# C of the first two token pairs: loaded in rows of 512 bytes and turned by VectorE, in a Mamba-2 scan with a feed-forward block

## The chip, the cores and the metric

The kernel runs on one core of a Trainium2 chip. The metric is the device time of one execution in microseconds, here the median of several runs. The core has five engines with a queue of instructions each: TensorE (PE in the profile; PEld is its weight load), VectorE (DVE), ScalarE (ACT), GpSimd (POOL) and SyncE (SP), which here only issues DMAs. SPq and ACTq are the queues of SyncE and ScalarE when they issue a DMA.

## What is computed

A selective state-space scan (Mamba-2) feeds a block of two matrix products with a leaky activation. Cut to what matters:

```python
# x (4, 8, 768, 32); a (4, 8, 768); B, C (4, 8, 768, 16): batch, heads, tokens, width
log_a = np.log(np.clip(a, 1e-06, 1.0))
for c in range(nc):                       # chunks of 32 tokens
    cum = np.cumsum(la, axis=-1)
    L = np.exp(cum[..., :, None] - cum[..., None, :]) * causal
    y_intra = einsum('bhij,bhjd->bhid', einsum('bhin,bhjn->bhij', Cc, Bc) * L, xc)
    y_inter = einsum('bhin,bhnd->bhid', Cc, state) * np.exp(cum)[..., None]
    y[:, :, sl] = y_intra + y_inter
    state = exp(sum la) * state + sum_j exp(cum[-1:] - cum)_j * B_j (x) x_j
h = y_as_(3072, 256) @ w_in               # (256, 2048)
g = np.maximum(h, 0.0) + alpha * np.minimum(h, 0.0)
out = g @ w_out                           # (2048, 256)
```

w_in and w_out arrive as 64-bit floats, which the kernel converts itself.

## The kernel before, in words

The 3072 tokens of all batches are cut into 24 chunks of 128, which are handled in twelve pairs; a group is four chunks, 512 tokens. For each pair the kernel loads B, C and x, forms the decays with scans on VectorE, the products of B and C ("gram") on TensorE, multiplies both, and adds up y from them and from the carried state. The feed-forward block goes over groups. All engines' orders are written out by hand: the order in which the Python code calls operations is the order in each engine's queue, and an engine whose next instruction has to wait holds everything behind it.

The start, up to some 27 us of the profile, is the function `first_two` (L821). It handles pairs 0 and 1 in chunks of 64 tokens, with the first weights' conversion and the first hidden products between them. In the order of the code:

- `load_pair(0)` (L235) issues the first loads. On SyncE: a for the pair (`ap`), B for the pair's two chunks (L192), x for both (L197), a of pair 1. On ScalarE's queue: the rows of a (L184), C for both chunks (L192), alpha. A load of B or C for one chunk takes 128 tokens into 128 partitions and, for each token, eight rows of 16 floats, one for each head: 1024 rows of 64 bytes, 64 KB.
- Two pieces of raw weights (`load_next`, L1435, issued by L257), 512 KB each, follow on SyncE.
- `rows_short` and `rows_out` send small products to DRAM, then `load_pair(1)` (L982) issues B, C, B, C (L192) and x, x (L197), and `load_second` (L983, issued by L231) reads back the products (`ap`).
- VectorE clamps a (L437), scans the rows (L493, L497), and scans the decays of pair 0 out of PSUM (L871, four scans), which TensorE has spread (L865).
- `turned` (L837) turns B and C of pair 0: four transposes on TensorE (L843), with tokens in the partitions before and head and state width after, into two banks, and two copies by ScalarE (L847), C first. `spread_c` (L851, L854) then makes `cz`, C masked by the head's parity, on ScalarE.
- alpha is turned and copied (L992, L994); GpSimd multiplies B by the decays (`bn`, L533).
- gram of pair 0 (L881) needs B's copy and `cz`; VectorE multiplies it into the decays (L887); TensorE adds up y (L929), the states (L895, L910, masked by GpSimd in L916) and their part of y (L941). `cd` (L961) is C times the decays, on GpSimd.
- VectorE and ScalarE convert the first raw piece of w_in (L296, L278, L308; L273, L283), GpSimd adds the halves (L330), and the first hidden products run (L1110).
- Pair 1 goes the same way, with the conversion of further pieces between its steps; its `turned` is at L1040 and its scans at L1029 to L1035, and its gram and y come between the matrix products of the second pair of hidden blocks (`among`, L1062).

Some short matrix products of constants (`keep_warm`, L335) fill TensorE's pauses at the start. Pairs 2 to 4 turn B and C on TensorE (L669). From pair 5 on (`turned` in `load_pair`, which is true from there), B and C are also loaded as blocks of 512 contiguous bytes, 8 tokens of one head to a partition (L210 to L217), and turned by VectorE in blocks of 32 by 32 (`turn_bc`, L571, L574).

The lines around the change in `first_two` are these:

```python
        rows_turn("short", prq)
        tp, hp = spare(), spare()
        bc0 = turned(nat0, (tp, hp), True)
        cz0 = spread_c(bc0)
```

Of the kernel before, what the change touches and what calls it, by code (L numbers as in the profile page):

```python
# [22 lines left out]
def kernel(  # L23
# [25 lines left out]
    nc = tc.nc  # L49
# [4 lines left out]
    batch, H, S, D = x.shape  # L54
    N = B.shape[-1]
    P = 128
    Q = 128
# [18 lines left out]
    NB = 2  # L76
# [20 lines left out]
    gp = ctx.enter_context(tc.tile_pool(name="gp", bufs=16))  # L97
# [6 lines left out]
    def bank(i):  # L104


        return ps_q.tile([P, 512], F32, name="bank", tag=f"q{i}")
# [15 lines left out]
    def load_rows(i, eng=nc.sync):  # L123

        rows = ld.tile([RW, Q], F32, name="rows")
        eng.dma_start(out=rows, in_=a.rearrange("b h (c t) -> (b h c) t", t=Q)[i * RW : (i + 1) * RW])
        loads["r", i] = rows
# [3 lines left out]
    def load_a(t, b, c, eng=nc.sync):  # L131
        first = a[b, 0:1, c * Q : (c + 2) * Q]
        eng.dma_start(out=t, in_=bass.AP(tensor=first.tensor, offset=first.offset,
                                             ap=[[S, H], [0, N], [1, 2 * Q]]))
# [4 lines left out]
    def load_tokens(dst, src, t0):  # L139


        d = dst.rearrange("p j (h w) -> p j h w", h=H)
        for k in range(2):
            for j in range(2):
                t = t0 + k * Q + j * HQ
                nc.sync.dma_start(out=d[HQ * k : HQ * (k + 1), j],
                                  in_=src[:, t : t + HQ, :].rearrange("h p w -> p h w"))

    def load_spread(gp, b, c):

        for w, t in enumerate(loads["p", gp][1] if gp >= HALF else ()):
            rows = scratch["z", b // 2].rearrange("(b h c) t -> b c h t", b=2, h=H)
            for k in range(2):
                nc.sync.dma_start(
                    out=t[HQ * k : HQ * (k + 1), : 4 * SQ].rearrange("p (h t) -> p h t", h=4),
                    in_=rows[b % 2, c + k, 4 * w : 4 * w + 4].unsqueeze(0)
                    .to_broadcast([HQ, 4, SQ]))
        for k, t in enumerate(loads["p", gp][1] if gp < HALF else ()):
            rows = scratch["z", b // 2].rearrange("(b h c) t -> b c h t", b=2, h=H)[b % 2, c + k]
            nc.sync.dma_start(out=t.rearrange("p (h t) -> p h t", h=H),  # L160
                              in_=rows.unsqueeze(0).to_broadcast([P, H, Q]))
            yield

    def load_products(gp, ap):
        b, c = divmod(2 * gp, CPB)
        rows = scratch["pf", b // 2].rearrange("(b h c) t -> b h (c t)", b=2, h=H)
        rows = rows[b % 2, :, c * Q : (c + 2) * Q]
        nc.sync.dma_start(out=ap, in_=rows.unsqueeze(1).to_broadcast([H, N, 2 * Q]))

    def load_pair(gp, decays=True, parted=False):  # L170


        b, c = divmod(2 * gp, CPB)
        turned = gp > GC
        nat = ldx.tile([P, 3, 2, H * N], F32, name="nat")
        xt = ldx.tile([P, 2, HD], F32, name="xt")

        ap = ldx.tile([P, 2 * Q], F32, name="ap")
        if gp == 0:
            load_a(ap, b, c)  # L180
        elif gp > NB:
            load_products(gp, ap)
        if gp == 0:
            load_rows(0, nc.scalar)  # L184
        abc = []
        if gp >= HALF:
            load_tokens(nat[:, 0], B[b], c * Q)
        def load_bc(k):
            ts = slice((c + k) * Q, (c + k + 1) * Q)
            for i, src in enumerate((B,) if turned else (B, C)):  # L190
                eng = nc.scalar if gp == 0 and i else nc.sync
                eng.dma_start(out=nat[:, i, k].rearrange("p (h n) -> p h n", h=H),  # L192
                              in_=src[b, :, ts, :].rearrange("h p n -> p h n"))

        def load_x(k):
            ts = slice((c + k) * Q, (c + k + 1) * Q)
            nc.sync.dma_start(out=xt[:, k].rearrange("p (h d) -> p h d", h=H),  # L197
                              in_=x[b, :, ts, :].rearrange("h p d -> p h d"))

        for k in range((1 if parted else 2) if gp < HALF else 0):  # L200
            load_bc(k)
            if gp >= NB:
                load_x(k)
        for k in range(2 if gp < NB else 0):
            load_x(k)
        if gp == 0:
            nc.scalar.dma_start(out=al_n, in_=moe_alpha.rearrange("(k p) -> k p", p=P))
            loads["a", 1] = prep.tile([P, 2 * Q], F32, name="a1")
            load_a(loads["a", 1], b, c + 2)
        for i, src in enumerate((B, C) if turned else ()):  # L210


            for e in range(2):
                first = src[b, e : e + 1, c * Q : (c + 2) * Q, :]
                nc.sync.dma_start(out=nat[:, 1 + e, i],
                                  in_=bass.AP(tensor=first.tensor, offset=first.offset,
                                              ap=[[2 * S * N, P // 32], [8 * N, 32], [1, 8 * N]]))  # L217
        for k in range(2 if gp >= NB else 0):
            abc.append(lda.tile([P, H * Q], F32, name="abc"))
        loads["p", gp] = nat, abc, xt, ap  # L220
        if gp >= HALF:
            load_tokens(xt, x[b], c * Q)
        if decays:
            for part in load_spread(gp, b, c):
                pass
        return lambda: load_bc(1), lambda: load_x(1)

    def load_second():

        rows = scratch["short", 0].rearrange("(b h c) t -> b h (c t)", b=2, h=H)  # L230
        nc.sync.dma_start(out=loads["p", 1][3], in_=rows[0, :, 2 * Q : 4 * Q].unsqueeze(1)  # L231
                          .to_broadcast([H, N, 2 * Q]))
# [102 lines left out]
    def keep_warm(to, n, cols=2 * Q):  # L335

        for i in range(n):
            nc.tensor.matmul(to[:, :cols], warm.to_broadcast([P, P]), warm.to_broadcast([P, cols]),
                             start=True, stop=True, skip_group_check=True)

    keep_warm(ps_h.tile([P, GT], F32, name="hp"), WARM, GT)
    ident = const.tile([P, P], F32, name="ident")
# [3 lines left out]
    for v in range(2):  # L346
        vs = slice(HQ * v, HQ * (v + 1))
        nc.vector.tensor_copy(out=ident_q[vs].rearrange("p (c t) -> p c t", c=4),
                              in_=ident[vs, vs].unsqueeze(1).to_broadcast([HQ, 4, HQ]))
# [196 lines left out]
    def spare():  # L546

        return ps_h.tile([P, GT], F32, name="hp", tag="hp")
# [272 lines left out]
    def first_two():  # L821
# [4 lines left out]
        nat0, _, xt0, ap0 = loads["p", 0]  # L826
# [7 lines left out]
              for i in range(2)]  # L834
        halves = [slice(HQ * j, HQ * (j + 1)) for j in range(2)]

        def turned(nat, banks, warmed=False):  # L837


            bc = work.tile([P, 4, Q], F32, name="bc")  # L840
            for k in range(2):
                for i, tp in enumerate(banks):
                    nc.tensor.transpose(tp[:, k * P : (k + 1) * P], nat[:, i, k], ident)  # L843
                if warmed and k == 0:
                    keep_warm(banks[0][:, 2 * Q :], 1)
            for i in (1, 0):
                nc.scalar.copy(out=bc[:, 2 * i : 2 * i + 2].rearrange("p k t -> p (k t)"),  # L847
                               in_=banks[i][:, : 2 * Q])
            return bc

        def spread_c(bc):  # L851
            cz = czp.tile([P, 2, 2, Q], F32, name="cz")
            for e in range(2):
                nc.scalar.mul(cz[:, e].rearrange("p k t -> p (k t)"),  # L854
                              bc[:, 2:].rearrange("p k t -> p (k t)"), par[:, e : e + 1])
            return cz
# [13 lines left out]
        def scan(i, r, t):  # L870
            nc.vector.tensor_tensor_scan(out=dec[i][:, r], data0=t[:, : 2 * Q], data1=ident_q,  # L871
                                         initial=0.0, op0=ALU.mult, op1=ALU.add)
# [27 lines left out]
        def dps_in(banks):  # L900
            return [t[:, 2 * Q : 2 * Q + 4 * D].rearrange("p (k m) -> p k m", k=2) for t in banks]
# [54 lines left out]
        def ss():  # L956
            return ps_s.tile([P, 512], F32, name="ss")
# [20 lines left out]
        sp = [bank(r) for r in range(4)]  # L978
# [3 lines left out]
        load_pair(1)  # L982
        load_second()  # L983
        nat1, _, xt1, pf1 = loads["p", 1]
        for r in range(4):
            scan(0, r, sp[r])
        rows_turn("short", prq)
        tp, hp = spare(), spare()
        bc0 = turned(nat0, (tp, hp), True)
        cz0 = spread_c(bc0)  # L990
        al_p = ss()
        nc.tensor.transpose(al_p[:, :NF], al_n, ident[:NF, :NF])  # L992
        keep_warm(al_p[:, Q:], 1, 3 * Q)
# [23 lines left out]
        sp = [bank(r) for r in range(4)]  # L1017
# [19 lines left out]
        convert_next(first=False)  # L1037
        own = [ss(), ss()]
        second = spare()
        bc1 = turned(nat1, (sp[0], second))  # L1040
        cz1 = spread_c(bc1)
        dps = dps_in(own)
        mask(0, slice(3, 4))
        slope_signs()
# [535 lines left out]
```

## Time and profile before

| What | Value |
|---|---|
| runs | 355.82, 355.99, 357.87 us; median 355.99 |
| the profiled execution: its span, first instruction to last | 355.9 us |
| busy: PE, DVE, ACT, POOL | 349.3, 235.8, 171.8, 204.4 us |
| DMA queue of SyncE (q1) | 103048 packets, 29.43 MB |
| DMA queue of ScalarE (q10) | 2496 packets, 0.32 MB |
| load of B or C, 64-byte rows, to issue (L192) | median 526 (B) and 592 ns (C) on SyncE, longest 3521 and 3890 |
| load of B or C, 512-byte rows, to issue (L215) | median 568 and 536 ns |
| VectorE's transpose of 128x512 (L574) | 1112 ns, median of 7 |
| ScalarE's copy of 128x256 out of PSUM (L847) | 373 ns |
| share of the chain that ended last: PE, SPq, DMA, DVE | 89, 4, 3, 2% |

A row of a timeline gives the start and duration in us, the engine, the line of the kernel, the operation, the tile written and the one read, its shape, how many instructions are merged into the row, and in brackets how long the engine was idle before it and what ended that. In a table by stage each engine's busy time in the stretch is followed by the number of its instructions; the last three columns are TensorE's granted clock (1.00 is full), the DMA engines' mean busy share and the GB/s moved. In a list of waits: who waited for whom, us in total, times, the longest.

### The profile page before, as it was taken

The numbers are of one execution on the slowest core, as the hardware profiler recorded it, in microseconds if no ns is written. First come the engines' busy times: TensorE is split into PE (matmuls) and PEld (weight loads), VectorE is DVE, ScalarE is ACT, GpSimd is POOL, SyncE is SP. The second block draws the span as 40 slices with busy tenths as digits, with TensorE's granted clock in tenths as the row PEclk, the third lists the DMA queues.
The fourth block names the chain that finished last, engine by engine and source line by source line (L and its number), as shares of the span: only waits on it lengthen the run. The fifth ranks groups of instructions, "written<-read, shape, count | busy, mean of one in ns | idle before, by whom it ended". The sixth has DMA issues, their size and how long they took to land.

```text
span 355.9 us, 7778 instructions
## 1 busy us (share of the span) xinstructions
PE 349.3 (98%) x2985; PEld 284.4 (80%) x2985; DVE 235.8 (66%) x482; ACT 171.8 (48%) x391; POOL 204.4 (57%) x228
## 2 busy tenths in 40 slices
PE   8899999999999999999999999999999999999996
PEld 4576665578788888888888888888888888888885
DVE  6876986998748756847747856757856633643363
ACT  3477576535355346345345445345445344443431
POOL 6776568589939855725646626637526535434520
PEclk9999999999999999999999999999999999999999
DMA  7899989607345403503423423422001001001102
GB/s 138 182 202 270 329 174 279 148 17 159 106 83 128 102 3 75 104 2 77 78 57 74 86 51 71 85 55 65 11 2 31 0 2 29 2 1 31 31 0 59
DMA packets 105581, 30.24 MB, mean 85 GB/s; under 512 B 79896, under 2 KB 101448, under 8 KB 105544
## 3 DMA queue, kind: packets, MB, share of 16 engines
q1 hardware_dynamic: 103048, 29.43, 36.3%
q10 hardware_dynamic: 2496, 0.32, 0.6%
q8 instruction: 23, 0.38, 0.5%
q14 instruction: 14, 0.11, 0.1%
HBM read 26.32 MB, written 3.42 MB: 84 GB/s over the span
## 4 chain that ended last, share of the span: by engine, by line
PE 89%; SPq 4%; DMA 3%; DVE 2%; ACT 1%; POOL 1%; issue 0%; DVEq 0%; ACTq 0%
PE bank L1216 33%; PE hp L1241 29%; PE bank L1142 6%; PE ss L1241 6%; PE hp L1095 3%; DMA raw<-in_moe_w_in_dram 2%; SPq L192 2%; PE ss L787 1%; PE ss L731 1%; PE hp L1110 1%; PE bank L1209 1%; PE ss L805 1%; PE ss L779 1%; DMA xt<-in_x_dram 1%; SPq L197 1%; PE ss L742 1%
## 5 line engine op out<-in xcount | busy, mean ns | idle before, releaser
L1298 POOL TENSOR_TENSOR gt<-gt 128x512 f32<-128x512 f32 x58 | 74.2, 1279 | 21.1 <-DVE gt L1226 16.3
L1216 PE MATMUL bank<-gt,w_out 128*128 128x256 f32 x320 | 83.5, 381 | 0.0
L1216 PEld LDWEIGHTS bank<-gt,w_out 128*128 128x128 f32 x320 | 60.1, 190 | 9.2 <-issue 1.0
L1288 POOL TENSOR_TENSOR gt<-gt 128x512 f32<-128x512 f32 x20 | 25.4, 1269 | 62.5 <-DVE gt L1226 49.7
L1226 DVE SCALAR_TENSOR_TENSOR gt<-hp,s_mul,gt 128x256 f32<-128x256 f32 x96 | 42.0, 479 | 29.1 <-ACT gt L1224 26.8
L1224 ACT ACTIVATE gt<-hp,s_alpha 128x256 f32<-128x256 f32 x96 | 40.3, 471 | 34.5 <-PE hp L1241 31.4
L1216 PE MATMUL bank<-gt,ws 128*128 128x256 f32 x224 | 55.9, 379 | 0.0
L1216 PEld LDWEIGHTS bank<-gt,ws 128*128 128x128 f32 x224 | 42.3, 190 | 5.6
L1241 PE MATMUL hp<-xs,w_in 128*128 128x256 f32 x160 | 41.9, 384 | 0.0
L1241 PE MATMUL hp<-xs,ws 128*128 128x256 f32 x160 | 41.1, 380 | 0.0
L1267 DVE TENSOR_TENSOR hp<-hp,u 128x512 f32<-128x512 f32 x20 | 14.0, 700 | 35.2 <-ACT u L1265 35.2
L1241 PEld LDWEIGHTS hp<-xs,ws 128*128 128x128 f32 x160 | 30.3, 190 | 4.3 <-POOL xs L1183 0.2
L1241 PEld LDWEIGHTS hp<-xs,w_in 128*128 128x128 f32 x160 | 29.7, 190 | 4.5
L1142 PE MATMUL bank<-w_out,gt 128*128 128x256 f32 x128 | 31.1, 385 | 0.4 <-POOL w_out L330 0.4
L1142 PEld LDWEIGHTS bank<-w_out,gt 128*128 128x128 f32 x128 | 23.6, 190 | 7.2 <-issue 2.9
L1241 PE MATMUL ss<-xT,w_in 128*128 128x256 f32 x96 | 24.6, 379 | 0.0
L645 POOL TENSOR_TENSOR sm<-state,bmask 128x256 f32<-128x256 f32 (+1 forms) x10 | 6.2, 620 | 29.0 <-DVE state L642 29.0
L1095 PE MATMUL hp<-xT,w_in 128*128 128x512 f32 x48 | 22.8, 596 | 0.0
L561 DVE TENSOR_TENSOR_SCAN dec<-abc,bank 128x192 f32<-128x192 f32 x48 | 22.7, 522 | 0.0
L1256 ACT COPY m<-hp 128x512 f32<-128x512 f32 x8 | 4.7, 586 | 35.7 <-PE hp L1241 35.7
L1265 ACT COPY u<-hp 128x512 f32<-128x512 f32 x20 | 11.7, 585 | 19.4 <-PE hp L1241 19.4
L1226 DVE SCALAR_TENSOR_TENSOR gt<-c,s_mul,gt 128x256 f32<-128x256 f32 x40 | 20.6, 555 | 0.0
(232 smaller groups left out, 608.2 us busy)
## 6 DMA issues: line engine op xcount, KB each, us to landing
abc<-z SPq DMA_DIRECT2D x24, 192.0 KB
raw<-in_moe_w_in_dram SPq DMA_DIRECT2D x8, 512.0 KB
raw<-in_moe_w_out_dram SPq DMA_DIRECT2D x8, 512.0 KB
abc<-z SPq DMA_DIRECT2D x8, 512.0 KB
out_dram<-o_sb SPq DMA_DIRECT2D x32, 64.0 KB
nat<-in_B_dram SPq DMA_DIRECT2D x26, 64.0 KB
xt<-in_x_dram SPq DMA_DIRECT2D x12, 128.0 KB
xt<-in_x_dram SPq DMA_DIRECT2D x24, 64.0 KB
```

The costliest lines, as they stand in the source:

```text
L192: eng.dma_start(out=nat[:, i, k].rearrange("p (h n) -> p h n", h=H), in_=src[b, :, ts, :].rearrange("h p n -> p h n"))
L561: nc.vector.tensor_tensor_scan(out=dv[:, o : o + SQ], data0=abc[k][:, s : s + SQ], data1=ident_p[0][:, :SQ], initial=0.0, op0=ALU.mult, op ...
L1095: nc.tensor.matmul(hp, w_in[:, k, f * P : (f + 1) * P], xts[g][:, k], start=(k == 0), stop=(k == KC - 1))
L1142: nc.tensor.matmul(pos[0][t // 2][:, t % 2], gt[:, t * Q : (t + 1) * Q], w_out[:, f], start=(f == 0 and t % 2 == 0), stop=(f == NF - 1), s ...
L1216: nc.tensor.matmul(ms[g][i][:, h], w, blocks[g, z][n][:, p], start=(q == 0 and h == 0), stop=(q == NQ - 1), skip_group_check=True)
L1224: nc.scalar.mul(o[:, p], h[:, p], s_alpha[:, fs[p]])
L1226: nc.vector.scalar_tensor_tensor(out=o[:, p], in0=h[:, p], scalar=s_mul[:, fs[p]], in1=o[:, p], op0=ALU.mult, op1=ALU.max)
L1241: nc.tensor.matmul(to[:, p], w(2 * z + p), b, start=start and p == 0, stop=True, skip_group_check=True)
L1265: nc.scalar.copy(out=u2, in_=A)
L1267: nc.vector.tensor_tensor(out=Y, in0=Y, in1=u2, op=ALU.add)
L1288: nc.gpsimd.tensor_tensor(out=tc_, in0=g22, in1=g12, op=ALU.subtract)
L1298: eng.tensor_tensor(out=o, in0=x0, in1=x1, op=ALU.subtract)
```

## The change

For pairs 0 and 1, C is no longer loaded by chunks in 64-byte rows but by `load_blocks`, two DMAs of 128 rows of 512 bytes each, as pairs 5 and later do. For pair 0 they stand where C's loads stood, on ScalarE's queue behind the rows of a; for pair 1 they go to SyncE's queue, now ahead of both loads of B. `turned` is split. `turned_c` turns C with one transpose on VectorE, straight from SBUF to SBUF; `turned_b` leaves B as it was: two transposes on TensorE and a copy on ScalarE. In pair 0, C is turned and spread ahead of the four scans and of `rows_turn`, so on VectorE the transpose stands between L497 and the scans L871, and on ScalarE the spreading comes ahead of the copy of `prt` (L511). In pair 1 the transpose stands on VectorE between the last scan L871 and L910; on ScalarE the spreading now comes ahead of B's copy. The number of DMAs stays the same. The line numbers below and in the prediction are those of the kernel before; the changed kernel's are up to nine higher.

```diff
@@ load_pair
-            for i, src in enumerate((B,) if turned else (B, C)):
-                eng = nc.scalar if gp == 0 and i else nc.sync
-                eng.dma_start(out=nat[:, i, k].rearrange("p (h n) -> p h n", h=H),
+            for i, src in enumerate((B,) if turned or gp < NB else (B, C)):
+                nc.sync.dma_start(out=nat[:, i, k].rearrange("p (h n) -> p h n", h=H),
                               in_=src[b, :, ts, :].rearrange("h p n -> p h n"))
...
+        def load_blocks(i, src, eng=nc.sync):
+            for e in range(2):
+                first = src[b, e : e + 1, c * Q : (c + 2) * Q, :]
+                eng.dma_start(out=nat[:, 1 + e, i],
+                              in_=bass.AP(tensor=first.tensor, offset=first.offset,
+                                          ap=[[2 * S * N, P // 32], [8 * N, 32], [1, 8 * N]]))
+
+        if gp < NB:
+            load_blocks(1, C, nc.sync if gp else nc.scalar)
         for k in range((1 if parted else 2) if gp < HALF else 0):
             load_bc(k)
...
@@ first_two
-        def turned(nat, banks, warmed=False):
+        def turned_c(nat):
             bc = work.tile([P, 4, Q], F32, name="bc")
+            nc.vector.transpose(
+                bc[:, 2:].rearrange("p k t -> p (k t)").rearrange("p (c b) -> p b c", b=8),
+                nat[:, 1:, 1].rearrange("p e (b n) -> p b e n", n=N))
+            return bc
+
+        def turned_b(bc, nat, bank, warmed=False):
             for k in range(2):
-                for i, tp in enumerate(banks):
-                    nc.tensor.transpose(tp[:, k * P : (k + 1) * P], nat[:, i, k], ident)
+                nc.tensor.transpose(bank[:, k * P : (k + 1) * P], nat[:, 0, k], ident)
                 if warmed and k == 0:
-                    keep_warm(banks[0][:, 2 * Q :], 1)
-            for i in (1, 0):
-                nc.scalar.copy(out=bc[:, 2 * i : 2 * i + 2].rearrange("p k t -> p (k t)"),
-                               in_=banks[i][:, : 2 * Q])
-            return bc
+                    keep_warm(bank[:, 2 * Q :], 1)
+            nc.scalar.copy(out=bc[:, :2].rearrange("p k t -> p (k t)"), in_=bank[:, : 2 * Q])
...
         nat1, _, xt1, pf1 = loads["p", 1]
+        bc0 = turned_c(nat0)
+        cz0 = spread_c(bc0)
         for r in range(4):
             scan(0, r, sp[r])
         rows_turn("short", prq)
         tp, hp = spare(), spare()
-        bc0 = turned(nat0, (tp, hp), True)
-        cz0 = spread_c(bc0)
+        turned_b(bc0, nat0, tp, True)
...
-        bc1 = turned(nat1, (sp[0], second))
+        bc1 = turned_c(nat1)
         cz1 = spread_c(bc1)
+        turned_b(bc1, nat1, sp[0])
```

More of the change, by code (lines that the diff above doesn't have):

```diff
@@ L210, in load_pair @@
         for i, src in enumerate((B, C) if turned else ()):
[L213 to L217, printed above, removed]
+            load_blocks(i, src)
         for k in range(2 if gp >= NB else 0):
```

## The prediction

> **What bounds the kernel now.** I read three views in this order: the table by stage, the waits of the first 50 us, and the order of time on VectorE and on SyncE's queue in the first 20 us. The table by stage comes first because it says how much there is to win. Its columns are the stretch, its length, and each engine's busy time.
>
> ```profile
> 0.00:9.00 9.00, 7.63 (x85) 3.68 (x91) 6.01 (x19) 3.03 (x7) 5.89 (x21) 1.00 0.80 140
> 9.00:18.00 9.00, 7.88 (x189) 5.44 (x190) 7.45 (x19) 4.16 (x12) 6.71 (x10) 1.00 0.88 183
> 18.00:27.00 9.00, 8.73 (x138) 6.84 (x139) 7.11 (x19) 6.36 (x17) 6.31 (x12) 1.00 0.92 199
> 27.00:46.00 19.00, 18.55 (x84) 11.17 (x83) 15.20 (x29) 12.34 (x25) 12.06 (x13) 1.00 0.94 285
> 46.00:80.00 34.00, 34.00 (x267) 22.37 (x268) 28.76 (x50) 19.02 (x37) 24.61 (x25) 1.00 0.62 157
> 80.00:350.00 270.00, 270.00 (x2218) 232.78 (x2217) 169.32 (x345) 125.91 (x294) 148.81 (x149) 1.00 0.25 53
> ```
>
> TensorE (first number) never rests between 46 and 350 us, at a granted clock of 1.00. The changed instructions all stand before 20 us. So the change works by starting that long run earlier or later. TensorE is idle 1.37 + 1.12 + 0.27 + 0.45 = 3.21 us before 46 us, of which 0.83 us come before its first instruction; 2.38 us can be won. The next view says who ends these pauses.
>
> ```profile
> PE hp L1110 <- POOL w_in L330: 0.9, 1, 0.9
> PE hp L338 <- PEq L1564: 0.8, 1, 0.8
> PE bank L881 <- ACT alpha L994: 0.5, 1, 0.5
> PE bank L1142 <- POOL w_out L330: 0.4, 1, 0.4
> PE bank L929 <- DVE dec L887: 0.3, 1, 0.3
> PE ss L895 <- DMA xt<-in_x_dram: 0.2, 1, 0.2
> ```
>
> Two of them lie on what the change touches: gram of pair 0 (L881) waits for ScalarE, which copies and spreads C, and the largest (L1110, 14.11) waits for the first weights. VectorE shows why these weights are late; the value in brackets is its idle time.
>
> ```profile
> 4.55 0.39 DVE L497 TENSOR_TENSOR_SCAN gt<-rq,gt 96x128 f32<-96x128 f32 x1
> 5.55 2.43 DVE L871 TENSOR_TENSOR_SCAN dec<-bank,ident_q 128x256 f32<-128x256 f32 x4 [0.61 <-PE bank L865]
> 7.90 0.67 DVE L1000 TENSOR_TENSOR_SCAN gt<-gt 128x256 f32<-128x256 f32 x1
> 8.97 0.76 DVE L887 TENSOR_TENSOR dec<-bank,dec 128x256 f32<-128x256 f32 x2 [0.40 <-PE bank L881]
> ```
>
> From 8.97 to 11.54 it works without a pause and then begins on the first raw weights (L296, 11.54), for which ScalarE (L273) also starts at 11.54, when they land. So two chains meet there: VectorE's own, and the DMA's. The last view is SyncE's queue.
>
> ```profile
> 2.74 2.32 SPq L197 DMA_DIRECT2D xt<-in_x_dram  x2
> 5.10 0.65 SPq L133 DMA_DIRECT2D a<-in_a_dram  x1
> 5.80 0.97 SPq L257 DMA_DIRECT2D raw<-in_moe_w_in_dram  x2
> ...
> 9.40 3.52 SPq L192 DMA_DIRECT2D nat<-in_B_dram  x1
> ```
>
> Loads of x take 1.28 and 0.99 us to issue at 2.74, and 0.58 each at 13.59 and 14.17: the queue is held up. A load of B at 9.40 holds it 3.52 us.
>
> **The change part by part.** The profiled execution spans 355.9 us, which lies 0.1 below the median of 355.99; I make the sum against the span.
>
> *Pair 0, ScalarE and TensorE.* Two transposes go from TensorE (0.11 us apart in the rows at 16.4) and one copy from ScalarE (0.37). One transpose of 128x256 comes to VectorE. Bounds of its price: 0.43 us from the 128x256 transpose at 348.75, and half of 1.11, so 0.56, from the seven of 128x512 at L574; these read the same strided blocks, so I take 0.56. In VectorE's order it stands between L497, which ends at 4.94, and the scans L871, which wait for TensorE until 5.55. The pause of 0.61 us covers it, if C has landed by 4.94. A load has no landing time in this trace; the nearest is rows of a, issued on the same queue at 0.81 and used at 3.71, so 2.9 us. The second block of C would be issued at about 1.85 and land at 4.75. The other bound is B's second load, issued at 2.12 and released to TensorE at 6.29, 4.2 us. I take 4.75: its queue neighbour is the nearer row, and the packets fall from 1024 to 128 a load.
>
> ScalarE then makes cz at 5.6 to 6.5 (0.92), before prt (0.24), B's copy (0.37) and alpha (0.17): gram is released at about 7.3 in place of 8.27. That is 1 us, of which VectorE can use 0.40: its scan L1000 ends at 8.57 and L887 began at 8.97. The prt copy slips from 5.79 to 6.5, and bn on GpSimd from 6.42 to about 6.8; its user, L895, stood behind gram at 8.93, so this costs nothing. The gram's last two banks still wait for the scans that end at 7.98. Gain on VectorE 0.40, so it reaches L296 at 11.14.
>
> *First weights.* C's two loads of pair 0 are 2048 packets of 64 bytes. The rows of the half microseconds from 14.0 to 15.0, just behind the 64-byte loads issued up to 13.5, move 107 to 110 GB/s, so 64 KB cost 0.6 us and both 1.2 us. From 36 to 42 us, where decay tables in 512-byte rows and weights move, it is about 400 GB/s: 0.33 us for both. So 0.9 us of DMA time go from ahead of the raw weights. SyncE's x loads lose up to 0.70 + 0.41 = 1.11 us of holding. The raw weights thus land between 0 and 1.1 us earlier than 11.5: nothing if the holding is x and B's own, 1.1 if it all goes. I take 0.8, nearest to the DMA time, so 10.7. ScalarE's step (0.67) then ends at 11.4, VectorE's L278 starts at 11.57 behind L296 instead of 12.24: gain 0.67, passed to L308, GpSimd's L330 and TensorE's L1110. If only 0.4 or less comes off the landing, the gain here is that much.
>
> *Pair 1, queue.* C goes ahead of B on SyncE; four issues stay four (0.53 to 0.57 each in the later block loads, so issue itself is no cheaper), past which x, ap and the third weights are moved. C of pair 1 falls from 2048 packets to 256. DMA is nearly idle from 12.0 to 13.5 (share 0.42, 0.19, 0.10), so x and ap, which end pauses at 17.54 and 18.30, should land over 1 us earlier. That uncovers the next limits, both on VectorE and GpSimd.
>
> *Pair 1, VectorE.* The second transpose (0.56) stands between the scans, which end at 17.57, and L910, which waited 0.72 us for ap. With everything 0.67 earlier: scans end 16.9, transpose 17.46, L910 at 17.5 instead of 18.30. Behind it L441 ends at 19.3. But ScalarE now gets C last: cz 17.5 to 18.4, then B's copy to 18.8, and gram starts at 18.8 against 19.31. It took 0.70 from gram's start to L887 in pair 0, so L887 starts at 19.5 against 20.08: gain 0.58. Behind the copy ScalarE holds L1120 (18.40, now 18.8) and the conversion L273 (19.58, now 19.65); GpSimd's next use of it is at 21.20, so it is covered. GpSimd's cd (L961, 9.18 and 19.02) now waits for VectorE's C, which is there at 5.6 and 17.5.
>
> *Sum.* 0.4 and 0.67 are stations of one chain, not added; at L929, from which TensorE runs to 45.4 with one pause (0.27 at 21.5, for the same L887), 0.58 is left, say 0.6. The pause at 45.4 (0.44) hangs on VectorE and a weight load that landed at 37.28; with the DMA earlier by more than 0.6 it does not grow. Span 355.3, median 355.4.
>
> **A rule against the change.** The Trainium skill, "VectorE: DVE Perf Modes", section "Rules for kernel authors", advises TensorE for a 128x128 transpose where PSUM may be the destination, which is what the kernel does before. The trace disagrees in part: TensorE's pair is cheaper (0.22 against 0.56) but needs the 0.37 us copy on ScalarE. By the rule, with neither transpose of 0.56 covered, 1.1 would be set against the 0.6 and the sum would be 0.5 slower; by the rows both stand in pauses.
> The same skill, "DMA: Bandwidth & Descriptors", section "Issuing engines are not separate DMA queues", says that transfers from all engines interleave on the same 16 DMA engines. No row here separates the two queues; by that statement C on ScalarE's queue delays the weights and my 0.8 stands, and without it the sum would be the first rival's.
>
> **The rivals.** *No change.* The weights still land at 11.5. Then L278 stays at 12.24, scans end at 17.57, the transpose ends at 18.13, L910 gains 0.15, cz runs to 19.1, B's copy to 19.5, and gram starts 0.2 later; L887 starts between 19.9 and 20.2. Time 355.8 to 356.2. For it: SyncE's holding may be due to x alone. Against: 0.9 us less DMA work.
> *Slower.* C of pair 0 lands late and VectorE, in order, holds four scans behind the transpose. Every 0.1 us after 4.94 shifts L887; it decides from 5.34 on, where the 0.40 is used up. At B's 6.29 the scans start 1.35 late, L887 at 9.9, L296 at 12.5: 0.95 slower, 356.9. Against: rows landed in 2.9 us on the same queue.
> *More.* The holding, x, ap and also the pause at 45.4 go: 0.6 + 0.44 + up to 0.5 of the remaining pauses, 354.4. Even with all 2.38 us and the four transposes (4 x 0.11) it is 2.8 us.
>
> **How the numbers follow.** Forecast (354.9 to 355.7) 0.48, no change (355.7 to 356.3) 0.22, slower (356.3 to 357.2) 0.14, more (under 354.9) 0.11, and 0.05 for a loss that no row here prices. The times shown spread from 355.82 to 357.87, so about 1% is what this kernel's measurement tells from no change. A gain over 1% (3.6 us) needs more than the 2.8 us there are: 0.02. A loss over 1% needs the slow rival nearly four times over, or a fall of the granted clock from 1.00: 0.05. Within 1%: 0.93. The range leaves out half of "more", the end of "slower" and the unpriced loss, some 0.16 in all: 354.3 to 356.8.
>
> **What would show it.** Right: ScalarE's queue at about 700 packets instead of 2496; a VectorE transpose of 128x256 ending by 5.55 and the scans still at 5.55; L887 at 8.6; the first L296 at 11.1; the long issue of 3.52 shorter; L929 of pair 1 near 20.0; granted clock 1.00 throughout. Wrong: the scans after 6.0; the first weights still at 11.5; gram of pair 1 later than 19.3 behind B's copy; a new pause of TensorE after 27 us that gives the gain back.

## The result and the profile after

The changed kernel takes 357.28 us, the median of 22 runs (357.02 to 359.30); the kernel before, in 22 runs of the same sessions, takes 356.41 us (355.69 to 358.14). The ratio is 1.0025, with a 95% interval from 1.0014 to 1.0036: about 0.9 us slower. That is within 1%, as given 0.93, but above the predicted range and on the other side of the forecast.

The execution profiled after took 357.31 us and spans 355.6 us. In all later runs too the time is some 1.7 us above the span. The span of 355.9 shown of before therefore belongs to an execution of about 357.6 us, some 1.2 above the median: spans must be compared with spans. In a second profiled execution of the unchanged kernel (the first experiment), the span is 355.1; over its twelve runs the median span is 354.45.

The table by stage of the changed kernel (columns as before: stretch and length, then busy time of TensorE, its weight loads, VectorE, ScalarE and GpSimd, granted clock, DMA share, GB/s):

```profile
0.00:9.00 9.00, 7.30 (x58) 3.46 (x62) 4.96 (x18) 2.66 (x6) 5.52 (x19) 1.00 0.64 131
9.00:18.00 9.00, 8.38 (x215) 5.72 (x208) 8.46 (x21) 3.38 (x9) 6.81 (x13) 1.00 0.80 178
18.00:27.00 9.00, 8.73 (x136) 6.38 (x137) 6.74 (x20) 6.51 (x17) 6.38 (x12) 1.00 0.91 212
27.00:46.00 19.00, 19.00 (x88) 11.89 (x87) 16.71 (x30) 12.76 (x26) 12.78 (x14) 1.00 0.96 288
```

The first 9 us are where VectorE does less: 4.96 against 6.01. The DMA share there falls from 0.80 to 0.64, and yet the work starts later. In the fourth row TensorE no longer pauses (19.00 against 18.55). The clock is 1.00 throughout. The line numbers in a view are those of the kernel that ran. VectorE's rows of pair 0 (start and duration in us, line, operation, tiles, in brackets the idle time before and what ended it):

```profile
4.69 0.40 DVE L500 TENSOR_TENSOR_SCAN gt<-rq,gt 96x128 f32<-96x128 f32 x1
6.62 0.64 DVE L843 STREAM_TRANSPOSE bc<-nat 128x256 f32<-128x256 f32 x1 [1.54 <-DMA nat<-in_C_dram]
7.11 2.37 DVE L876 TENSOR_TENSOR_SCAN dec<-bank,ident_q 128x256 f32<-128x256 f32 x4
9.40 0.70 DVE L1006 TENSOR_TENSOR_SCAN gt<-gt 128x256 f32<-128x256 f32 x1
10.02 0.73 DVE L892 TENSOR_TENSOR dec<-bank,dec 128x256 f32<-128x256 f32 x2
...
12.64 0.42 DVE L299 TENSOR_SCALAR wr<-raw 128x512 uint32<-128x512 uint32 x1
...
18.04 0.62 DVE L843 STREAM_TRANSPOSE bc<-nat 128x256 f32<-128x256 f32 x1
18.51 0.91 DVE L915 SCALAR_TENSOR_TENSOR gt<-gt,ap,ss 128x64 f32<-128x64 f32 x3
...
20.74 1.42 DVE L892 TENSOR_TENSOR dec<-bank,dec 128x256 f32<-128x256 f32 x4 [0.99 <-PE bank L886]
```

The new transpose waits 1.54 us for C. The four scans behind it need nothing of C, and start at 7.11 instead of 5.55 all the same, because VectorE works in order. From there the delay is handed on: first product at 10.02 (8.97 before), first raw weights at 12.64 (11.54). At pair 1 the wait of 0.72 us for `ap` ahead of the states' step is gone (18.51 directly follows the transpose), but the transpose took its place, and the product now waits 0.99 us for gram. The chain of waits of the changed kernel, from its start (start, length, what), says the same:

```profile
1.25 1.15 ACTq L203
2.40 0.03 issue
2.43 4.09 DMA nat<-in_C_dram
...
6.62 0.64 DVE bc L843
7.26 0.54 DVE dec L876 x2
```

ScalarE needs 1.15 us to issue the first block of C, the second starts at 2.43, and its data is there 4.09 us later. TensorE's waits of the first 50 us (total, count, longest):

```profile
PE hp L341 <- PEq L1571: 0.8, 1, 0.8
PE bank L886 <- ACT bc L854: 0.8, 1, 0.8
PE hp L1117 <- POOL w_in L333: 0.4, 1, 0.4
```

Gram of pair 0 (L886) now waits for B's copy (L854). The wait for the converted w_in went from 0.9 to 0.4, and the one for w_out at 45 us is no longer there. SyncE's queue:

```profile
2.83 2.46 SPq L196 DMA_DIRECT2D xt<-in_x_dram  x2
5.33 1.07 SPq L133 DMA_DIRECT2D a<-in_a_dram  x1
6.45 0.97 SPq L260 DMA_DIRECT2D raw<-in_moe_w_in_dram  x2
...
9.65 3.64 SPq L191 DMA_DIRECT2D nat<-in_B_dram  x2
```

The queue is held no less: the issue of x takes 2.46 (2.32 before), that of `a` 1.07 (0.65), so the raw weights are issued at 6.45 instead of 5.80. The page's section on queues gives ScalarE's queue, q10, 680 packets instead of 2496, so the change does what it says.

### The profile page after: what moved, and what is told of

The parts are those of the page before. It is cut to its first block, busy times and chain, and to the rows that moved or that the text cites. A ratio compares the mean times of both kernels' runs of the same rounds, so it can differ in the third digit from the quotient of the medians.

```text
span 355.6 us, 7771 instructions
## 1 busy us (share of the span) xinstructions
PE 349.5 (98%) x2981; PEld 284.4 (80%) x2981; DVE 236.7 (67%) x484; ACT 171.4 (48%) x389; POOL 205.1 (58%) x228
## 4 chain that ended last, share of the span: by engine, by line
PE 95%; DVE 1%; DMA 1%; ACT 1%; ACTq 0%; issue 0%; POOL 0%; DVEq 0%
PE bank L1223 33%; PE hp L1248 29%; PE bank L1149 8%; PE hp L1102 6%; PE ss L1248 6%; PE ss L790 1%; PE ss L734 1%; DMA nat<-in_C_dram 1%; PE bank L1216 1%; PE ss L808 1%; PE ss L782 1%; PE hp L1117 1%; DVE dec L876 1%; PE ss L745 1%; PE ss L621 1%; PE bank L1117 0%
```

## The experiments

The first theory after the result: the wait for C, put ahead of the scans in VectorE's order, is the whole loss. Its rivals: the transposes' own time, pair 1, or the shape of C's rows. A second question was why C came at 6.5 and not at 4.75.

### The kernel before once more

No edit.

> The kernel before, unchanged. It tells what lies outside the span of an execution and how typical the first profile is. The changed kernel's runs lie 1.7 us above their spans; if the same holds here, the execution profiled before (span 355.9) took about 357.6 us, and a typical one spans about 354.7. Ratio 1.000 within 0.001 either way.

356.19 against 356.29 us, ratio 1.0003 [0.9987, 1.0019]. Its VectorE rows:

```profile
4.55 0.40 DVE L497 TENSOR_TENSOR_SCAN gt<-rq,gt 96x128 f32<-96x128 f32 x1
5.02 2.43 DVE L871 TENSOR_TENSOR_SCAN dec<-bank,ident_q 128x256 f32<-128x256 f32 x4
...
8.94 0.76 DVE L887 TENSOR_TENSOR dec<-bank,dec 128x256 f32<-128x256 f32 x2 [0.91 <-PE bank L881]
...
11.43 0.42 DVE L296 TENSOR_SCALAR wr<-raw 128x512 uint32<-128x512 uint32 x1
11.77 0.42 DVE L278 TENSOR_SCALAR wt<-wt 128x512 f32<-128x512 f32 x1
...
19.36 1.42 DVE L887 TENSOR_TENSOR dec<-bank,dec 128x256 f32<-128x256 f32 x4
```

and ScalarE's first conversion:

```profile
10.56 0.67 ACT L273 ACTIVATE wt<-raw 128x512 f32<-128x512 f32 x1 [0.87 <-DMA raw<-in_moe_w_in_dram]
```

Without any change the first weights were here at 10.6, not 11.5, L278 followed VectorE's own L296 without a wait, and the product of pair 1 came at 19.36 instead of 20.08. The pause of 0.61 ahead of the scans is gone too (5.02 instead of 5.55), so a transpose there would have had no cover even with C in time; in two later profiles with pair 0 as before it is 0.71 and 0.32. Two terms of the forecast were read from one execution's chance.

### Only pair 0, only pair 1

In each, one pair is loaded and turned as in the changed kernel, the other as before:

```diff
-            for i, src in enumerate((B,) if turned or gp < NB else (B, C)):
+            for i, src in enumerate((B,) if turned or gp == 0 else (B, C)):
```

(and `gp == 1` in the other).

> Only pair 0 is changed; pair 1 is loaded and turned as before. Theory: the loss comes from VectorE, which stands before the four scans until C lands at 6.5 us. Then all of it is here: scans of pair 0 start at 7.1, ratio 1.002 to 1.004. Rival (the loss is pair 1's, where B's copy now stands behind the spreading of C): ratio 0.998 to 1.000.

> Only pair 1 is changed; pair 0 as before. Theory (the loss is pair 0's late C): ratio 0.998 to 1.000, scans of pair 0 at 5.5. Rival (B's copy behind the spreading delays gram of pair 1): ratio 1.002 to 1.004, with gram of pair 1 later than at 19.3.

Pair 0 alone: 357.10 against 356.29, ratio 1.0025 [1.0007, 1.0043], the whole change's ratio. Its profile has the same wait, and the first product 0.95 later than in the kernel before:

```profile
6.49 0.64 DVE L858 STREAM_TRANSPOSE bc<-nat 128x256 f32<-128x256 f32 x1 [1.48 <-DMA nat<-in_C_dram]
...
9.89 0.72 DVE L907 TENSOR_TENSOR dec<-bank,dec 128x256 f32<-128x256 f32 x2
```

Pair 1 alone: 356.69, ratio 1.0014 [1.0000, 1.0027]. A loss between nothing and 0.3%, between what the theory and the rival gave, and not the gain of 0.6 us. Nor is it clear that pair 1 makes it: in this profile the first product of pair 0, which is as before, starts at 9.66, against 8.94 to 8.97 in the other three profiles of such a pair 0 without the copy tried below. VectorE's rows of its pair 1:

```profile
16.39 1.26 DVE L891 TENSOR_TENSOR_SCAN dec<-bank,ident_q 128x256 f32<-128x256 f32 x2
17.57 0.62 DVE L858 STREAM_TRANSPOSE bc<-nat 128x256 f32<-128x256 f32 x1
...
20.27 1.42 DVE L907 TENSOR_TENSOR dec<-bank,dec 128x256 f32<-128x256 f32 x4 [1.00 <-PE bank L901]
```

From the end of the scans (17.65) to the product are 2.62 us; in the two profiles of before they are 2.51 and 2.43. The wait for `ap` that goes is paid back by the transpose and by what follows it: `cz` first, then B's copy, then gram. The losses of the two kernels, 0.81 and 0.40 us, do not add to the 0.87 of the whole, but their intervals allow it.

### The transpose two scans later

C's transpose of pair 0 goes between the second and the third scan, and `cz` behind B's copy:

```diff
-        bc0 = turned_c(nat0)
-        cz0 = spread_c(bc0)
-        for r in range(4):
+        for r in range(2):
+            scan(0, r, sp[r])
+        bc0 = turned_c(nat0)
+        for r in range(2, 4):
             scan(0, r, sp[r])
...
         turned_b(bc0, nat0, tp, True)
+        cz0 = spread_c(bc0)
```

> The changed kernel, but in pair 0 VectorE turns C between the second and the third scan, and ScalarE spreads it behind prt and B's copy. Theory: VectorE's wait of 1.5 us goes, its first product with gram starts near 9.2 instead of 10.0, ratio against the kernel before 0.999 to 1.001. Rival (pair 1, or VectorE's extra 0.6 us wherever it stands): ratio 1.002 to 1.004, as the changed kernel.

356.44 against 356.29, ratio 1.0005 [0.9993, 1.0017]. Loads, transposes and copies are those of the changed kernel; only the place differs:

```profile
6.87 0.61 DVE L843 STREAM_TRANSPOSE bc<-nat 128x256 f32<-128x256 f32 x1
...
9.18 0.76 DVE L892 TENSOR_TENSOR dec<-bank,dec 128x256 f32<-128x256 f32 x2
```

No wait stands in brackets now, though the transpose runs at nearly the same time as before (6.87 against 6.62), because two scans fill the time. The product is at 9.18 rather than 10.02, and the loss is gone as far as the interval tells (it leaves up to 0.6 us). So the transposes' own time and the loads are not the loss; the place is. ScalarE's order was changed along with it. In the changed kernel gram started at 8.65, and with the 0.70 us that passed before from gram's start to the product, ScalarE's order alone would allow a product at about 9.35 (an estimate): it can hold at most 0.4 of the 1.05 us by which the product came later, the rest is VectorE's wait.

### A copy that only waits

The kernel before, with 64-byte rows and TensorE's transposes, gets a copy on VectorE of one column of each chunk's C ahead of the four scans; nobody uses it.

```diff
+        probe = prep.tile([P, 2], F32, name="probe")
+        nc.vector.tensor_copy(out=probe, in_=nat0[:, 1, :, 0])
         for r in range(4):
             scan(0, r, sp[r])
```

> The kernel before, with one more VectorE copy of one column of each chunk's C (128x2) where the changed kernel has the transpose. It makes VectorE wait there for C in 64-byte rows and so shows its landing. Theory A (C lands late at this place whatever its rows, since it shares the DMA engines with B and x): the copy waits until 6.0 to 7.0 us. Theory B (the 512-byte rows land later than the 64-byte rows did): the copy runs by 5.5 and the scans start where they did.

> The kernel before with the one-column copy of C on VectorE ahead of pair 0's scans, timed. Theory (the wait at this place is the whole loss, not the transpose and not the rows): ratio 1.002 to 1.004, as the changed kernel. Rival (the early wait is absorbed and the loss is the transposes' VectorE time): ratio 0.999 to 1.001.

A first run took 357.41 us. Twelve runs of the same kernel take 357.30 against 356.15, ratio 1.0031 [1.0016, 1.0047]. VectorE in the second profile:

```profile
6.89 0.17 DVE L986 COPY probe<-nat 128x2 f32<-128x2 f32 x1 [1.47 <-DMA nat<-in_C_dram]
...
9.94 0.72 DVE L887 TENSOR_TENSOR dec<-bank,dec 128x256 f32<-128x256 f32 x2
```

With a copy of 0.17 us in place of the transpose the loss is as large, so the transpose's price isn't needed for it. But these executions don't show that VectorE's wait alone makes it. TensorE's rows, first in the kernel before and then in the first run with the copy:

```profile
6.29 0.44 PE L843 MATMUL hp<-ident,nat 128*128 128x128 f32 x2
8.27 0.73 PE L881 MATMUL bank<-cz,bc 32*64 32x128 f32 x32 [0.53 <-ACT alpha L994]
```

```profile
7.18 0.44 PE L843 MATMUL hp<-ident,nat 128*128 128x128 f32 x2 [0.54 <-DMA nat<-in_B_dram]
```

B's second chunk came 0.9 us late, in the timed kernel too (7.20), and gram started at 9.16 and 9.17 instead of 8.27. With 0.70 from gram to the product that makes about 9.87 without any wait on VectorE (an estimate), against 9.94 measured. Both ways lead to the same loss, and why B is late there is open.

C in 64-byte rows was usable on VectorE at 6.89 here and at 6.75 in the first run, the 512-byte rows at 6.5 to 6.6: at most 0.4 us earlier. Even that may belong to these executions alone: in the kernel before, the two transposes from 6.29 on are those of the second chunks of B and C, so TensorE was done with C in 64-byte rows by 6.73. The shape of the rows does not make C late.

### What makes C late: four kernels

Four kernels, one profiled run each, change what is in flight at the start. First, C's blocks stand ahead of the rows of a on ScalarE's queue:

```diff
+            load_blocks(1, C, nc.scalar)
             # the load of the rows of a follows
```

> The changed kernel with C of pair 0 issued ahead of the rows of a on ScalarE's queue. Theory A1 (C waits behind B's and x's small packets): issued 0.4 us earlier and ahead of B's, it lands near 4, and VectorE's transpose does not wait for it, though the rows of a land later. Theory A2 (about 4 us pass from the end of the issue to the landing whatever stands ahead): the transpose still waits until about 6.

Now the rows, issued at 2.61, were late:

```profile
6.59 0.22 DVE L441 TENSOR_SCALAR rq<-rows 96x128 f32<-96x128 f32 x1 [2.80 <-DMA rows<-in_a_dram]
...
7.74 0.62 DVE L844 STREAM_TRANSPOSE bc<-nat 128x256 f32<-128x256 f32 x1
```

C was there before 7.74, but when cannot be read, since VectorE stood at the rows: inconclusive on C. Yet a small load that took 2.9 us as the first of its queue took 4.0 as the third. Next, x of pair 0 is loaded behind both pieces of raw weights:

```diff
-        for k in range(2 if gp < NB else 0):
+        if gp == 0:
+            loads["x0"] = load_x
+        for k in range(2 if gp == 1 else 0):
...
+    for k in range(2):
+        loads["x0"](k)
```

> The changed kernel with x of pair 0 issued behind both first weight loads on SyncE's queue, so that no load of x is in flight when C lands. If x's packets keep C back, the transpose of pair 0 starts by 5.5 instead of 6.6; if B's do, or nothing does, it stays between 6.2 and 6.8. Its total time is not compared, since x itself comes late.

```profile
6.52 0.64 DVE L845 STREAM_TRANSPOSE bc<-nat 128x256 f32<-128x256 f32 x1 [1.58 <-DMA nat<-in_C_dram]
```

C came no earlier. But without x SyncE issued the raw weights at 4.57 instead of 6.45, so they were in flight beside C in x's place: x by itself is not separated. Then B of pair 0 goes behind the weights too:

```diff
-            load_bc(k)
+            if gp:
+                load_bc(k)
...
+    for load in loads["bx0"]:
+        for k in range(2):
+            load(k)
```

> The changed kernel with B and x of pair 0 issued behind both first weight loads, so that C is issued with only a's loads and the weights around it. If B's small packets ahead of it keep C back, VectorE's transpose of pair 0 starts by 5.2; if it is the time that any load issued there takes, it stays near 6.5. Its total time is not compared, since B and x come late.

```profile
8.34 0.64 DVE L846 STREAM_TRANSPOSE bc<-nat 128x256 f32<-128x256 f32 x1 [3.40 <-DMA nat<-in_C_dram]
```

C comes 1.7 us later, not earlier. With B and x behind them, SyncE issues the weights at 2.33 instead of 6.45, and C, whose second block ScalarE's queue issues at 2.43, is late although it stands on another queue. The Trainium skill, "DMA: Bandwidth & Descriptors", section "Issuing engines are not separate DMA queues", states that transfers of all issuing engines run on the same 16 DMA engines and interleave; this delay of 1.7 us agrees. What B's small packets alone do is not separated, since the weights came in their place, and B and x followed at 3.33 and 5.09. Last, SyncE is held behind its first load until C has landed, by a copy of a column of C as VectorE's first instruction and a store of that column ahead of B's loads:

```diff
+            nc.vector.tensor_copy(out=seen, in_=nat[:, 1:, 1, 0])
+            sent = dr.tile([P, 2], F32, name="sent")
+            nc.sync.dma_start(out=sent, in_=seen)
```

> The changed kernel with SyncE's queue held behind its first load until C of pair 0 has landed: a VectorE copy of one column of C (128x2) stands first on VectorE, and a store of that copy to DRAM ahead of B on SyncE. Only the rows of a and ap are then in flight beside C. If other traffic keeps C back, the copy runs by 4.8 (2.9 us from issue to use, as the rows of a, counted from about 1.9); if a load issued there takes 4 us by itself, near 6.5. Its total time is not compared, since all else comes late.

```profile
5.74 0.17 DVE L211 COPY seen<-nat 128x2 f32<-128x2 f32 x1 [5.74 <-DMA nat<-in_C_dram]
```

The table by stage of this run, and under it half a microsecond of the kernel before, just behind the issue of 64-byte rows of B and C:

```profile
3.00:4.00 1.00, 1.00 (x2) 0.01 (x1) 0.00 (x0) 0.47 (x1) 0.06 (x1) 1.00 0.23 70
4.00:5.00 1.00, 0.59 (x1) 0.00 (x0) 0.00 (x0) 0.81 (x1) 0.00 (x0) 1.00 0.26 73
5.00:6.00 1.00, 0.00 (x0) 0.00 (x0) 0.26 (x2) 0.00 (x0) 0.00 (x0) 1.00 0.04 11
```

```profile
14.00:14.50 0.50, 0.39 (x2) 0.37 (x3) 0.50 (x3) 0.50 (x1) 0.50 (x2) 1.00 1.12 107
```

C is usable at 5.74, some 0.9 earlier than in the changed kernel and still 0.8 after VectorE would need it. ScalarE's two issues end at 2.97, so 2.8 us pass after the last one. Most of that is the transfer itself: some 154,000 bytes move from 3 to 6 us, of which by the sizes of the loads C's two blocks are 131,000 (an estimate), at 70 and 73 GB/s and a DMA share of about a quarter, four engines' worth of 16. From 84.0 to 85.5 us of the kernel before, where SyncE has just issued only such blocks of B and C, it is the same: 76 to 86 GB/s at a share of 0.26 to 0.29. Behind the 64-byte rows it is 107 GB/s at a share of 1.12. So in this form of load the longer rows keep fewer engines busy and, with little beside them, move no faster. Whether that comes from the outermost count of four in the blocks' access pattern (`P // 32` in the diff) no run tried. Taking nearly all other loads away does not bring C, at this place of its queue, to 4.94.

### B's copy ahead of cz in pair 1

Two kernels copy B of pair 1 before `cz`, so that gram waits for one step less behind the transpose. The first has the late transpose of pair 0 as well, the second changes pair 1 alone:

```diff
         bc1 = turned_c(nat1)
+        turned_b(bc1, nat1, sp[0])
         cz1 = spread_c(bc1)
-        turned_b(bc1, nat1, sp[0])
```

> As the variant in which VectorE turns C of pair 0 between the second and third scan, and in pair 1 ScalarE copies B ahead of the spreading of C, in its pause. If B's copy behind the spreading is what delays gram of pair 1, gram starts 0.35 us earlier and the ratio against the kernel before is 0.998 to 1.000; if gram is held by the matrix products ahead of it, 1.000 to 1.001 as without this edit.

> Only pair 1 is changed, and ScalarE copies its B ahead of the spreading. If B's copy was what pair 1's change cost, ratio 0.999 to 1.001; if gram of pair 1 hangs on the matrix products ahead of it, no gain either, so not under 0.998; if it stays at 1.001 to 1.003 the cost of pair 1 lies elsewhere.

With the late transpose: 356.27 against 356.03, ratio 1.0006 [0.9993, 1.0019]. Pair 1 alone: 356.49 against 356.15, ratio 1.0009 [0.9993, 1.0024]. In the latter the scans end at 17.01 and the product starts at

```profile
19.44 1.42 DVE L907 TENSOR_TENSOR dec<-bank,dec 128x256 f32<-128x256 f32 x4 [0.80 <-PE bank L901]
```

which is 2.43 us, as in the kernel before. In the former, TensorE's rows show what gram then stands behind:

```profile
17.99 1.10 PE L1119 MATMUL hp<-xT,w_in 128*128 128x256 f32 x4
19.02 0.72 PE L886 MATMUL bank<-cz,bc 32*64 32x128 f32 x32
```

Gram follows the hidden products without a gap, and these wait for the w_in that GpSimd converts. So the order gives back the 0.2 us of pair 1, and no more. No kernel tried here beats the kernel before by what the measurement can tell.

## Why the prediction was wrong

**The step that failed** is "The second block of C would be issued at about 1.85 and land at 4.75". It was usable at 6.62, 1.87 us later. The run with little else in flight splits that: the second issue starts at 2.43, not 1.85 (0.58, as the first takes 1.15 us), from there to use it takes 3.3 instead of 2.9 even so (0.4), and the other traffic adds 0.9. The 2.9 us came from the rows of a, the first load of that queue, 48 KB (no wait stands ahead of their use at 3.71, so they may have landed earlier still), and "its queue neighbour is the nearer row" chose wrongly: B's second load, 4.2 us from issue, was the nearer (4.2 here too, from 2.43 to 6.62). The run with C first shows it on the rows themselves, 4.0 us as the third load. The reason given, 128 packets a load instead of 1024, did not help: the blocks moved at some 70 GB/s with little else in flight, where the sum of the weights took 400 GB/s from the decay tables.

**The rival "Slower"** names the mechanism, and its numbers are close: L887 at 9.9 (10.02 measured), L296 at 12.5 (12.64), 0.95 us slower (0.87 by the medians). It had a chance of 0.14. Its deciding point of 5.34 was passed by 1.3 us (6.62).

**First weights, 0.67.** The landing at 11.5 that this was read from belonged to the one profiled execution; at 10.6, in another of the same kernel, VectorE's own chain ends last and there is nothing to gain. SyncE's queue was not released either ("SyncE's x loads lose up to 0.70 + 0.41" of holding: x took 2.46 instead of 2.32). The reason given for the weights, fewer packets ahead of them, is right in the packets (680; about 700 said) and in the DMA share (0.64), but did not shorten the queue's issues.

**Pair 1, 0.6.** The wait for `ap` went, as said. Inside the pair the stations were right too: from the end of the scans to the product 2.6 us were said (16.9 to 19.5), and 2.62 measured (18.12 to 20.74). But before it was 2.51, so the pair itself had no gain in the sum: the 0.58 was the 0.67 of the weights, which was not there to win, less 0.09. Gram at 19.97 instead of 18.8 is the same 1.2 us by which the scans end later than said. Measured by itself, pair 1 changes nothing or loses up to 0.3%; with B's copy first it takes as long as before.

**The transpose's price**, 0.56, was 0.64 and 0.62: too low, but of little weight, as the run with the transpose two scans later shows. **The base:** "lies 0.1 below the median" set a span against a time. The two differ by 1.7 us, and the profiled execution was a long one.

**The pause at 45.4.** Said not to grow; it went. In the kernel before, TensorE waits 0.44 there in both profiles. In the changed kernel the work arrives later, and the wait is gone (19.00 busy of 19.00). The product of pair 1 is 1.38 later than in the second profile of before (20.74 against 19.36); less the 0.44 that makes 0.94, about the 0.87 measured. For the late transpose it makes 0.59 - 0.44 = 0.15, as measured; for pair 0 alone (20.96) 1.16 against 0.81 measured, and for the waiting copy (20.47) 0.67 against 1.15; for pair 1 with B's copy first (19.44) it makes -0.36 against 0.34. So the sum fits only within 0.7 us, which is as large as the losses themselves; that the pause takes up part of the delay is argued, not shown.

**Open:** why C's blocks move at only some 70 GB/s with the DMA engines three quarters idle, and which of the start's other loads adds the 0.9. Weights beside C make it worse; x and B alone were not separated.

## What to carry to other kernels

Before moving an in-order engine's use of a load ahead of work that doesn't need it, find when the load is usable at that place in its queue: a tiny copy put there costs nothing to write, and here it stood until 6.75 and 6.89 where the forecast had 4.75. A first load of a queue is no measure for the third; count each issue ahead of it, and the traffic. Take the rate of a load from loads of the same form, not only of the same row length. Make a sum from what two profiled executions agree on, and compare spans with spans.

## What the runs showed of the hardware

- The first of C's two block issues on ScalarE's queue took 1.15 us, the two together 1.72; the first profile of before has 0.53 to 0.57 each for such loads later on, on SyncE.
- At the start, 128 KB of C in 512-byte rows were usable at 6.5 to 6.6 us and in 64-byte rows at 6.75 to 6.89, with 680 against 2496 packets on the queue: an eighth of C's packets bought at most 0.4 us.
- Blocks of 512-byte rows moved at 70 to 73 GB/s at a DMA share of 0.23 to 0.26 in the run with C alone, and at 76 to 86 GB/s and 0.26 to 0.29 from 84.0 to 85.5 us of the kernel before; just behind 64-byte rows it was 107 to 110 GB/s and 1.10 to 1.12 there, from 14 to 15 us.
- Two weight loads of 512 KB issued on SyncE from 2.33 us on, beside C's two blocks on ScalarE's queue (1.25 and 2.43), and B and x behind them, moved C from 6.6 to 8.3 us.
- VectorE turns 128x256 of float32 in 0.61 to 0.64 us from these strided blocks.
- Two executions of the same kernel had the first weights at 11.5 and at 10.6 us, with spans of 355.9 and 355.1.
